# Output stores of a gated-attention and expert kernel: from SyncE's queue to GpSimd's

## The chip, the cores and the metric

The kernel runs on one core of one Trainium2 chip. The metric is the device time of one execution in microseconds (us), lower is better; the number given is the median of several executions. Beside it there is one profiled execution, taken by the hardware profiler, from which all rows of this document come.

The engines are named as the profile names them: PE is TensorE (matmuls), PEld its weight loads, DVE is VectorE, ACT is ScalarE, POOL is GpSimd, SP is SyncE. SP and POOL each have a queue of DMAs of their own; the packets of both are moved by the core's 16 DMA engines.

## What is computed

Two stages, one behind the other, with B = 8 sequences of S = 3072 tokens, width D = 256, 64 score channels and an inner width of 1024:

```python
scores = (1.0 / S) * np.matmul(z, z.transpose(0, 2, 1))
attn = np.maximum(scores, 0.0) ** 2
x = (u * np.matmul(attn, v)).reshape(B * S, D)
h1, h2 = x @ w1, x @ w2
out = np.maximum(h1, h2) @ w_out          # float32, 24576 x 256
```

The kernel uses max(h1, h2) = relu(h1 - h2) + h2, so it needs one inner product with w1 - w2 and a folded matrix w2 @ w_out.

## The kernel before, in words

**Steps.** Each sequence has six groups of 512 query tokens (`G` = 4 blocks of 128). The 48 (sequence, group) pairs are the steps, numbered n = 0 to 47. A step computes score tiles (PE), relu (ACT or DVE) and square (ACT or DVE) into `a_sb`, and from them the product with v in PSUM banks `acc0` and `acc1`. Because the scores are symmetric, a tile computed for one group is turned by a DMA transpose on SP's queue (`aT<-a_sb`, helper `turn`, L277) and read by a later step of the same sequence. The products of steps 3 and up are Strassen-like: seven half-size products in place of eight, with sums made by DVE (`es`, `lf`, `gs`, `xs`, `e`).

**The order on PE within a step n >= 3** is written out by hand (L1336 to L1389): the output products of step n-3 (`LAG` = 3, L49), named `o` 0 to 3; the inner products of step n-2, named `da`/`db` 0 to 3; and the step's own products in two phases, X and Y, each in two halves: `Xa`, `Xb`, `Ya`, `Yb`, each running over the six groups. `o` 0 opens the step, `Xb` with `o` 3 lies in its middle, `db` 3 lies between `Ya` and `Yb`, and `Yb` ends it. Score tiles of later steps are laid in between.

**Marks.** PE works with two halves of its rows side by side; before the halves swap banks, PE has to wait for its own earlier matmuls. This goes by way of POOL: `mark` (L93) puts an instruction on POOL that waits for the newest matmul, and a later matmul waits for it (`fence`, L87). POOL's queue is in program order, so whatever stands ahead of a mark in that queue delays it, and PE with it. There are 384 marks. In a step the last ones are that of `da` 3 and that at the end of `Ya` (L720, awaited by the first `Yb`); the next one comes behind `o` 0 of the following step (L1048).

**Loads** of u, v and z (`load`, L106) are DMAs of POOL's queue, in two parts of 64 rows each, 128 KB apiece for u and v. Each part waits for a chosen place in PE's order (`spot`, L1624): 0 is the first group of `Xa`, 1 that of `Xb`, 2 `da` 2, 3 the first group of `Ya`, 4 `db` 3, 5 the last group of `Yb`. In two steps of each sequence the two parts of the next u stand at places 4 and 5 (`U_SPOTS`, L1621).

**The output of a step** is made in `add_seven` (L968) for n = 3 to 46: ACT writes `o_sb` (L1078) after `o` 1, DVE and ACT finish it after `o` 3 (`oe0` on DVE by L296, `oe2` on ACT by L293), and job `store` (L1091) sends 512 KB, 128 partitions of 4 KB, to `out`. All this happens three steps after the step's own number. `o_sb` has two buffers (L74), so step n+2 writes the buffer that step n's store reads.

**The planner.** What runs on SP, POOL, ACT and DVE, and in which order, comes from a list scheduler (`find_orders`, L1861). Each `job` has the engines that may run it with a cost, jobs it depends on (`deps`), jobs that must only have begun (`after`), buffers it takes and uses, and a due time worked back from PE's order (`find_dues`). `share_wide` (L1938) gives the large tiles (`a_sb`, `aT`) their slots by the planned times. The planner's order is then written out and kept (`pin`).

Of the kernel before, what the change touches and what calls it, by code (L numbers as in the profile page):

```python
# [11 lines left out]
def kernel(  # L12
# [17 lines left out]
    nc = tc.nc  # L30
# [11 lines left out]
    G = 4  # L42
# [6 lines left out]
    LAG = 3  # L49
# [29 lines left out]
    pin = tc.keep_in_program_order  # L79
# [22 lines left out]
    def sp_dma(**kw):  # L102
        pin(nc.sync.dma_start(**kw))
# [134 lines left out]
    def tile_of(pool, key):  # L238
        return bufs[pool, key].tile
# [25 lines left out]
    steps = [Step(n, *divmod(n, NG)) for n in range(B * NG)]  # L265
# [702 lines left out]
    def add_seven(st):  # L968
        n, b, c = st.n, st.b, st.s
        xT, ok, sk, xk = ("xT", n), ("o", n), ("gs", n), ("xs", n)  # L970
# [109 lines left out]
        for name, ways, fn, deps, after, new, uses in (  # L1080
# [9 lines left out]
        out_b = out[ds(b * S, S), :].rearrange("(p t) d -> p t d", p=P)  # L1090
        job(  # L1091
            ("store", n),
            {"SP": 1300},
            lambda _: sp_dma(out=out_b[:, ds(c * G, G), :], in_=tile_of(*ok)),
            deps=[("oe2", n), ("oe0", n)],
            uses=[ok],
            lag=3000,
        )


    def add_second(st, split):
# [110 lines left out]
        if st.seven:  # L1212
            add_seven(st)
            return
# [92 lines left out]
    last = len(steps) - 1  # L1307
# [123 lines left out]
    for name in "s20 a10 s21 b10 a11 a12 b11 a13 s22 b12 b13 s23 a00 a01 s10 b00 b01 s11 a02 a03 b02 b03 s12 o00 s13 o01 o02 o03".split():  # L1431
        n, i = last - int(name[1]), int(name[2])
# [121 lines left out]
    def at_step(b, s, us):  # L1554
        return pe_job_at(starts[NG * b + s] + us * 1000)
# [121 lines left out]
    for dc in range(KD):  # L1677
# [7 lines left out]
            after=[("w2T", 0)] if dc else (),  # L1685
# [8 lines left out]
        after=at_step(0, 2, 6),  # L1694
# [390 lines left out]
```

## Time and profile before

| | |
|---|---|
| median of 3 executions | 885.39 us (884.83 to 885.87) |
| the profiled execution's own time | 889.46 us |
| its span, first to last instruction | 887.7 us |
| mean granted TensorE clock over the span | 0.998 |
| matmuls, marks, stores from SP | 16589, 384, 51 |

The profiled execution's own time is 1.76 us more than its span: 889.46 - 887.7. The profile is read from the engine that has no idle time, here PE, to the waits of the others.

### The profile page before, as it was taken

To read this page: it belongs to the slowest core of one execution; us is meant where nothing else is said; L and a number is where in the kernel's file an instruction comes from. 1 tells how busy PE (TensorE), PEld (TensorE's weight loads), DVE (VectorE), ACT (ScalarE), POOL (GpSimd) and SP (SyncE) were. 2 spreads that over 40 slices of the span, in tenths; PEclk is the share of its full clock that TensorE was granted. 3 is DMA by queue.
4 is the path that set the end of the run, shared out by engine and by line. 5 is a ranking of instruction groups with operands and counts; after the bars stand their busy time and mean duration, and the time that the engine had idled before them with its cause. 6 is when DMAs were issued, how large, how long until landed. Compare 5 with 4: busy or idle time off the path is not lost.

```text
span 887.7 us, 37934 instructions
## 1 busy us (share of the span) xinstructions
PE 879.5 (99%) x16589; PEld 718.3 (81%) x16589; DVE 804.6 (91%) x1721; ACT 753.0 (85%) x951; POOL 105.5 (12%) x218
## 2 busy tenths in 40 slices
PE   9999999999999999999999999999999999999998
PEld 4468888888888888788888888888888887788886
DVE  6877799999999999889999999999999999999984
ACT  8967998899978999689997899978999799987634
POOL 2101101111011110011101111011101111000000
PEclk9999999999999999999999999999999999999999
DMA  9999999997999989999999998999999999996621
GB/s 157 190 141 175 216 189 187 187 185 130 177 175 200 163 132 177 168 187 166 135 183 173 203 158 138 185 178 197 156 145 170 181 181 168 172 178 118 115 74 73
DMA packets 382310, 146.18 MB, mean 165 GB/s; under 512 B 360640, under 2 KB 362304, under 8 KB 382144
## 3 DMA queue, kind: packets, MB, share of 16 engines
q1 hardware_dynamic: 364128, 114.01, 79.4%
q0 software_dynamic: 18016, 29.75, 24.5%
q8 instruction: 129, 2.11, 1.0%
q14 instruction: 37, 0.30, 0.1%
HBM read 59.77 MB, written 25.17 MB: 96 GB/s over the span
## 4 chain that ended last, share of the span: by engine, by line
PE 97%; DVE 1%; DMA 1%; issue 0%; ACT 0%; POOL 0%; POOLq 0%; ACTq 0%
PE acc L86 50%; PE s_ps L86 47%; DMA z_sb<-in_z_dram 1%; ACT g_sb L282 0%; DVE zT L130 0%; DVE gs L299 0%; PE tpz_c L129 0%; ACT w2T_sb L293 0%; PE w2t_ps L1674 0%; DVE e L296 0%; DVE e L299 0%; DVE o_sb L296 0%; DVE w2T_sb L293 0%; DVE o_sb L299 0%; ACT o_sb L293 0%
## 5 line engine op out<-in xcount | busy, mean ns | idle before, releaser
L86 PEld LDWEIGHTS <-v_sb 64*128 64x128 bf16 x4552 | 327.9, 94 | 68.1 <-issue 4.3
L282 ACT ACTIVATE a_sb<-s_ps 128x1024 bf16<-128x1024 f32 (+1 forms) x334 | 302.2, 941 | 29.5 <-PE s_ps L86 26.3
L86 PEld LDWEIGHTS <-lf 64*128 64x128 bf16 x3240 | 260.1, 94 | 21.3 <-POOLq L94 3.3
L86 PE MATMUL acc<-es,v_sb 64*128 64x256 bf16 x2160 | 275.5, 269 | 0.0
L86 PE MATMUL acc<-es,lf 64*128 64x256 bf16 x1080 | 245.7, 269 | 0.0
L86 PE MATMUL acc<-a_sb,lf 64*128 64x256 bf16 x1224 | 229.8, 269 | 0.2 <-issue 0.2
L86 PE MATMUL s_ps<-xT,w_sb 64*128 64x512 bf16 (+1 forms) x1504 | 211.3, 377 | 0.1
L288 ACT ACTIVATE a_sb<-a_sb 128x1024 bf16<-128x1024 bf16 (+1 forms) x224 | 206.9, 953 | 1.5
L282 ACT ACTIVATE g_sb<-s_ps 128x1024 bf16<-128x1024 f32 x187 | 185.8, 1022 | 18.9 <-PE s_ps L86 16.8
L86 PE MATMUL acc<-aT,lf 64*128 64x256 bf16 x936 | 175.8, 269 | 0.0
L86 PE MATMUL acc<-a_sb,v_sb 64*128 64x256 bf16 (+2 forms) x1424 | 139.2, 284 | 0.3
L86 PE MATMUL s_ps<-zT 64*128 64x512 bf16 (+2 forms) x774 | 117.8, 333 | 0.3 <-DVE zT L130 0.2
L86 PEld LDWEIGHTS <-gs 64*128 64x128 bf16 x2816 | 100.1, 94 | 13.4 <-issue 3.1
L296 DVE TENSOR_TENSOR es<-aT 128x1536 bf16<-128x1536 bf16 (+1 forms) x117 | 106.2, 930 | 0.6
L107 POOL DMA_DIRECT2D u_sb<-in_u_dram x92 | 47.6, 517 | 430.6 <-PE acc L86 262.9
L86 PEld LDWEIGHTS <-w_sb 64*128 64x128 bf16 (+1 forms) x1520 | 74.2, 94 | 28.3 <-issue 1.7
L86 PEld LDWEIGHTS <-g_sb 64*128 64x128 bf16 x2304 | 85.8, 94 | 11.5 <-POOLq L94 7.4
L299 DVE TENSOR_TENSOR es<-a_sb 128x512 bf16<-128x512 bf16 x198 | 78.3, 419 | 17.1 <-PE acc L86 16.1
L290 DVE TENSOR_TENSOR a_sb<-a_sb 128x1024 bf16<-128x1024 bf16 (+1 forms) x112 | 74.2, 669 | 17.8 <-ACT a_sb L282 17.6
L86 PE MATMUL s_ps<-wf_sb,gs 64*128 64x128 bf16 x2112 | 84.6, 216 | 2.0 <-issue 1.9
L86 PE MATMUL acc<-aT,v_sb 64*128 64x256 bf16 x936 | 85.3, 269 | 0.0
L107 POOL DMA_DIRECT2D v_sb<-in_v_dram x89 | 46.1, 520 | 247.4 <-PE acc L86 133.8
(94 smaller groups left out, 1186.2 us busy)
## 6 DMA issues: line engine op xcount, KB each, us to landing
out_dram<-o_sb SPq DMA_DIRECT2D x47, 512.0 KB, 4.7
u_sb<-in_u_dram POOLq DMA_DIRECT2D x88, 128.0 KB, 4.2
v_sb<-in_v_dram POOLq DMA_DIRECT2D x82, 128.0 KB, 4.2
aT<-a_sb SPq DMA_TRANSPOSE x228, 5.0
z_sb<-in_z_dram POOLq DMA_DIRECT2D x12, 192.0 KB, 5.0
v_sb<-in_v_dram POOLq DMA_DIRECT2D x7, 256.0 KB, 6.8
u_sb<-in_u_dram POOLq DMA_DIRECT2D x4, 256.0 KB, 6.5
w_sb<-in_moe_w_dram POOLq DMA_DIRECT2D x2, 512.0 KB, 6.5
```

The source lines that it names most:

```text
L86: newest[0] = pin(nc.tensor.matmul(*args, **kw)).ins
L107: dma = pin(nc.gpsimd.dma_start(**kw))
L282: pin(nc.scalar.activation(out_ap, in_ap, AF.Relu))
L288: pin(nc.scalar.activation(ap, ap, AF.Square))
L290: pin(nc.vector.tensor_mul(ap, ap, ap))
L296: pin(nc.vector.tensor_add(*args))
L299: pin(nc.vector.tensor_sub(*args))
```

## The change

Three lines of the job `store` in `add_seven`. For steps with n + 3 < 47, that is n = 3 to 43, the store's engine is POOL instead of SP, so the DMA is issued by `nc.gpsimd`. It depends on the same two jobs as before; in addition it may be planned only once the second group of `Yb` of step n + 3 has begun in the plan. That is a rule for the planned order alone: the built DMA waits for no matmul. The stores of n = 44 to 46, of the three first steps and of the last step stay with SP.

```diff
         job(
             ("store", n),
-            {"SP": 1300},
-            lambda _: sp_dma(out=out_b[:, ds(c * G, G), :], in_=tile_of(*ok)),
+            {"POOL" if n + LAG < last else "SP": 1300},
+            lambda eng: pin((nc.gpsimd if eng == "POOL" else nc.sync).dma_start(out=out_b[:, ds(c * G, G), :], in_=tile_of(*ok))),
             deps=[("oe2", n), ("oe0", n)],
             uses=[ok],
+            after=[("Yb", n + LAG, steps[n + LAG].groups[1])] if n + LAG < last else [],
             lag=3000,
         )
```

In the built program 41 stores of 51 stand in POOL's queue and 10 in SP's. The order of all instructions on PE, DVE and ACT is the same as before, and so is the order of POOL's loads; on SP, besides the stores that left, two transposes of one early step have changed places. Some `a_sb` and `aT` tiles lie in other slots, because the planned times moved. On POOL each moved store stands directly behind the mark that ends `Ya`, or behind the load part that waits for `db` 3 where there is one, and ahead of the mark of the next step's `o` 0.

## Prediction

> **What bounds the kernel now.** I read the page first: which engine has no idle time, and what the DMA queues carry.
>
> ```profile
> span 887.7 us, 37934 instructions
> PE 879.5 (99%) x16589; PEld 718.3 (81%) x16589; DVE 804.6 (91%) x1721; ACT 753.0 (85%) x951; POOL 105.5 (12%) x218
> q1 hardware_dynamic: 364128, 114.01, 79.4%
> q0 software_dynamic: 18016, 29.75, 24.5%
> q8 instruction: 129, 2.11, 1.0%
> ```
>
> PE is busy 879.5 of 887.7 us; POOL is busy for 12%. SP's DMAs are queue q1, POOL's are q0, and q8 is the fetch of instructions: 129 packets, 2.11 MB, on the same DMA engines. A busy PE need not be a PE at its peak, so the second view is the table of waits:
>
> ```profile
> PE s_ps L86 <- issue: 1.9, 1, 1.9
> PE acc L86 <- issue: 0.2, 1, 0.2
> PEld L86 <- POOLq L94: 13.2, 77, 0.2
> DVE es L299 <- DMA aT<-a_sb: 1.0, 1, 1.0
> ```
>
> Behind the first few microseconds PE is idle hardly at all, and never for a DMA, a store or a turn; its longest idle time, 1.9 us, waits for nothing that the profile shows ("issue"). The marks cost weight loads 0.2 us at most. Of DVE's waits for turned tiles one is left, 1.0 us. Whether PE keeps its own pace is seen in the third view, the chain of waits in order of time. One run of 56 products comes once in each step at the same place:
>
> ```profile
> 226.91 2.84 PE s_ps L86 x56
> 334.52 2.84 PE s_ps L86 x56
> 371.66 1.92 issue
> 445.60 2.84 PE s_ps L86 x56
> 552.91 2.84 PE s_ps L86 x56
> 660.22 2.84 PE s_ps L86 x56
> 678.38 2.84 PE s_ps L86 x56
> 786.65 2.84 PE s_ps L86 x56
> ```
>
> These are starts, and neighbours are a sequence (six steps) apart, but for 660.22 to 678.38, which is one step. 445.60 to 552.91 and 552.91 to 660.22 are both 107.31 us, to the last digit. 226.91 to 334.52 is 107.61, 0.30 more; 678.38 to 786.65 is 108.27, 0.96 more; 334.52 to 445.60 is 111.08, 3.77 more, and there stands the 1.92 us of "issue". Behind it the granted clock falls:
>
> ```profile
> 373.60:377.00 3.40, 3.40 (x34) 1.97 (x36) 2.20 (x7) 2.13 (x3) 0.00 (x0) 0.53 1.13 212
> ```
>
> 3.40 us at a clock of 0.53 lose 3.40 x 0.47 = 1.60 us; with 1.92 that is 3.52 of the 3.77. So the steady part runs at PE's own pace with 0.30 + 3.77 + 0.96 = 5.03 us on top. The profiled execution's own time is 889.46; without the 3.77 it is 885.69, which is 0.30 above the median of 885.39. I take it that the timed executions lack this one stall. Without all 5.03 us it would be 884.43: the change can win about 885.39 - 884.43 = 0.96 us, unless it shortens the head or PE's own work, which it does not touch.
>
> **Part 1, what leaves SP.** 41 of 51 stores leave SP's queue.
>
> ```profile
> L103 SPq DMA_DIRECT2D out_dram<-o_sb x51: 332/518/1510, 87.8 to 884.6; - x51
> out_dram<-o_sb SPq DMA_DIRECT2D x47, 512.0 KB, 4.7
> ```
>
> Each took SP a median 0.518 us to issue and 4.7 us to land; 41 x 0.518 = 21 us of SP's time go, and the turns behind a store that waits for its output move up. Worth: 0. It would be worth something if PE, or an engine that holds PE up, waited for a turn; the only such wait is DVE's 1.0 us above, and PE's row has none. Bounds: no loss, and a gain of up to the 0.96 us above if all that is over the pace comes from the stores. I take 0, because nothing names them.
>
> **Part 2, what POOL gains.** 41 issues of 512 KB, 128 rows of 4 KB. No such DMA is in the trace, so the nearest rows are POOL's loads:
>
> ```profile
> L107 POOL DMA_DIRECT2D u_sb<-in_u_dram x92: 515/515/583, 4.2 to 848.0; - x92
> L107 POOL DMA_DIRECT2D v_sb<-in_v_dram x89: 515/515/599, 2.1 to 748.9; - x89
> L107 POOL DMA_DIRECT2D w_out_sb<-in_moe_w_out_dram x1: 894/894/894, 33.9 to 33.9; - x1
> w_out_sb<-in_moe_w_out_dram POOLq DMA_DIRECT2D x1, 512.0 KB, 7.7
> v_sb<-in_v_dram POOLq DMA_DIRECT2D x7, 256.0 KB, 6.8
> ```
>
> The issue costs 0.515 (64 rows of 4 KB) to 0.894 us (1024 rows of 1 KB). Seven of the v loads have the store's 128 rows and lie within the 0.599 maximum, so I take 0.6, or 41 x 0.6 = 25 us on an engine that idles 782. Landing takes 6.8 to 7.7 us by the 256 and 512 KB loads; I take 7.
>
> What waits behind the store on POOL is the mark of the next step's `o` 0, and PE waits for that mark. The store itself waits for DVE's last sum and ACT's last copy of its output. One step in full, for the store of n = 18; the second row counts marks in the window 397.5 to 402.4 and gives the first and the last:
>
> ```profile
> 395.99 0.41 DVE L296 TENSOR_TENSOR o_sb<-o_sb,s_ps 128x256 f32<-128x256 f32 x1
> L94 POOLq EVENT_SEMAPHORE  x2: 17/17/17, 397.9 to 402.3; - x2
> 398.63 0.52 POOL L107 DMA_DIRECT2D u_sb<-in_u_dram  x1 [2.96 <-PE s_ps L86]
> 402.06 0.60 PE L86 MATMUL s_ps<-xT,w_sb 64*128 64x512 bf16 x4
> L293 ACT COPY o_sb<-s_ps x2: 372/372/372, 393.6 to 411.5; 128x256 f32<-128x256 f32 x2
> L1078 ACT ACTIVATE o_sb<-s_ps x2: 597/597/597, 403.5 to 421.5; 128x512 f32<-128x512 f32 x2
> ```
>
> ACT is done at 393.6 + 0.37, DVE at 396.40, POOL reaches the store at 398.63 + 0.52 = 399.15. So the store finds both ready and leaves at once, early in `Yb`. It is done at 399.75; `o` 0 ends and `da` 0 starts at 402.06, and the mark follows at 402.3. Until 402.06 there are 2.91 us for an issue of 0.6. The margin is narrowest at the last moved store, n = 43 (first row below: POOL's load ends at 845.89, `da` 0 starts at 848.35: 2.46 us). The output is ready latest, against POOL, at the first, n = 3: DVE ends it at 124.93, 1.07 before the mark at 126.0 that stands ahead of the store.
>
> ```profile
> 845.37 0.52 POOL L107 DMA_DIRECT2D u_sb<-in_u_dram  x1 [13.38 <-PE s_ps L86]
> 848.35 0.59 PE L86 MATMUL s_ps<-xT,w_sb 64*128 64x512 bf16 x4
> 124.52 0.41 DVE L296 TENSOR_TENSOR o_sb<-o_sb,s_ps 128x256 f32<-128x256 f32 x1
> L94 POOLq EVENT_SEMAPHORE  x2: 17/17/17, 126.0 to 130.3; - x2
> ```
>
> So the marks come as before: 0. The cover is PE's own work in `Yb` and `o` 0; without it each store would cost its 0.6 us, 25 us in all. The store reads its `o_sb` from 399.75 to about 407; ACT writes that buffer again two steps on, at 421.5: 0.
>
> A rule of the Trainium skill speaks against this move. "SBUF — State Buffer", section "SBUF: two separate sides", says that descriptors of DMAs issued from GpSimd are written by its own cores, and that VectorE in a two-port mode locks them out; the same page's example has 620 ns become about 3100. By it the issue might take 0.6 x 5 = 3.0 us, past the 2.46. The trace does not bear it out here: beside a DVE that is busy 91%, none of 181 loads of u and v took over 0.599 us.
>
> **Part 3, the transfers.** The same 21 MB move on the same engines, but beside the turns instead of between them. In two steps a sequence, the second part of the next u is issued on POOL's queue some 2 us behind the store, and SP's `uT` waits for it. Behind a 512 KB store it may land up to 7 us later; `uT` and the turns behind it then go later. In the step above:
>
> ```profile
> uT<-u_sb SPq DMA_TRANSPOSE x48, 5.1
> 406.18 1.23 SPq L103 DMA_TRANSPOSE uT<-u_sb  x1
> 421.41 0.69 DVE L303 SCALAR_TENSOR_TENSOR xT<-e,uT 128x512 bf16<-128x512 f32 x1
> ```
>
> At worst `uT` starts at 413.2 and lands at 418.3, still 3.1 us ahead of DVE's use of it at 421.41. I take 0. Bounds: 0, and 3 us at each of these 14 steps, if turns behind a late `uT` became what PE waits for. The tiles in other slots get their data from the same instructions in the same order; I cost that at 0 too, covered by the same lack of waits on PE.
>
> **Sum.** 889.46 + 0 + 0 + 0 = 889.46 with this execution's stall, 885.69 without; against the median, 885.39 + 0, or **885.4 us**.
>
> **Rivals.**
>
> *A, instructions come late (slower).* The "issue" stall at 371.66 is what a late fetch on q8 would look like: PE stands still, no semaphore is awaited, and q8's 16 KB packets (2.11 MB / 129) share engines with q0 and q1. A store on q0 puts a third busy queue beside the turns and the fetch, 41 times for some 7 us. It decides from the point at which a fetch comes after PE has used up what it holds. Price: 3.77 us each, as measured. One in the median execution gives 885.39 + 3.77 = 889.2. For it: the stall exists, at a moment when the DMA engines were loaded. Against it: one in 129 fetches, although loads on q0 already meet turns everywhere. Chance 0.13.
>
> "DMA: Bandwidth & Descriptors", section "Queues, rings and completion order", of the Trainium skill says that each DMA engine goes round the queues that have work, packet by packet: a third one lengthens a fetch's wait. "Runtime: NRT & Kernel Launch", section "Instruction fetch mechanics", calls the cost of such a block mostly hidden, which 128 of 129 packets here agree with.
>
> *B, marks behind the store (slower).* If an issue takes more than 2.9 us in most steps, each excess goes to PE 41 times: at 3.3 us, 41 x 0.4 = 16 us, 902. Against it: 0.599 at most. Chance 0.05.
>
> *C, late u (slower).* 14 x 1 us gives 899. Against it: no DMA wait on PE. Chance 0.03.
>
> *D, the stall goes (faster).* If the timed executions too hold a stall of 3.77 us and the store on SP brings it on, the time falls to 885.39 - 3.77 = 881.6. Against it: 885.69 fits the median without it. Chance 0.05.
>
> That the change does not do what it says is excluded: in the built order 41 stores are POOL's.
>
> **How the numbers follow.** The forecast has 0.74. Its own range is 884.4 (all 0.96 won) to 886.4 (as much lost again to small fetch waits). 0.74 is not enough for the range, so it reaches on to A: 884.4 to 889.2, with 0.87. A difference of 0.2%, 1.8 us, is about what a measurement can tell from none: 883.6 to 887.2. Faster is D, 0.05; slower is A, B and C, 0.21; the same, 0.74.
>
> **What would show it.** In the profile after: 41 POOL rows `out_dram<-o_sb` of about 0.6 us; the wait for L94 still at 0.2 us at most; runs of 56 products 107.31 us apart; POOL near 130 us. A: new "issue" waits on PE, with a fallen clock behind them. B: store rows over 2.4 us and longer waits for L94. C: waits of SP for u beyond 407 and PE or ACT waiting for `aT`. D: an execution without any "issue" wait and well under 884. I am wrong if PE has a row of waits that is not in the list above.

## The result, and the profile after

The changed kernel takes 891.51 us (median of 13 executions, 887.62 to 900.1) against 886.55 for the kernel before on the same chip (13 executions, 884.15 to 891.89): a ratio of 1.0058, 95% interval 1.0039 to 1.0077. It is slower by 0.58%, some 5 us. The forecast was 885.4, and 891.5 lies above the range (884.4 to 889.2). Of the 6.1 us between them 1.2 are the start of the sum: it began at 885.39, the median of three executions of the kernel before, and thirteen give 886.55. The intervals in this document are over undisturbed executions; a profile is one execution, so a single pause in it is a draw.

The changed kernel's profiled execution took 890.09 us. First its page:

```profile
span 888.3 us, 37957 instructions
PE 877.8 (99%) x16589; PEld 741.8 (84%) x16589; DVE 804.8 (91%) x1721; ACT 753.6 (85%) x951; POOL 128.9 (15%) x259
q1 hardware_dynamic: 358224, 92.52, 73.4%
q0 software_dynamic: 23920, 51.25, 29.9%
q8 instruction: 129, 2.11, 1.0%
out_dram<-o_sb POOLq DMA_DIRECT2D x41, 512.0 KB, 5.2
```

21.5 MB have gone from q1 to q0, and POOL's busy time rose from 105.5 to 128.9 us: 23.4 us for 41 issues. A row of the groups by line shows them alone:

```profile
L1094 POOL DMA_DIRECT2D out_dram<-o_sb x41: 566/566/575, 127.7 to 845.5; - x41
```

0.57 us each, as reckoned (0.6). The waits of TensorE and its weight loads, in the same execution:

```profile
PE acc L86 <- DVE e L296: 1.3, 1, 1.3
PE s_ps L86 <- issue: 1.0, 2, 0.7
PE acc L86 <- issue: 0.6, 2, 0.4
PE acc L86 <- POOLq L94: 0.3, 1, 0.3
PEld L86 <- POOLq L94: 13.7, 78, 0.5
PEld L86 <- issue: 13.3, 36, 1.6
```

Where before had one "issue" wait of 1.9 us and one of 0.2 there are four small ones, one mark that comes late by 0.3 to 0.5 us, and one sum of DVE. The DVE wait lies at 112.75 us, before the first moved store (127.7), and up to there the order on every queue is as before. Behind it stands a load of v:

```profile
DVE lf L296 <- DMA v_sb<-in_v_dram: 1.2, 1, 1.2
```

That load landed 8.2 us behind its issue, 4.2 us in before's profile. PE stands at the same place, for 0.5 to 1.7 us, in nine of the twenty profiles of this case, one of them with all stores on SyncE's queue. So no moved store is its direct cause, but how often it comes in executions without a profile is not known. TensorE's pace is read from the chain, as before:

```profile
228.73 2.84 PE s_ps L86 x56
336.56 2.84 PE s_ps L86 x56
437.15 4.79 issue
444.37 2.84 PE s_ps L86 x56
553.05 2.84 PE s_ps L86 x56
660.52 2.84 PE s_ps L86 x56
768.04 2.84 PE s_ps L86 x56
```

Before, a sequence without pauses took 107.31 us. Now they take 107.83, 107.81, 108.68, 107.47 and 107.52: every sequence has lost something, 2.76 us in all five. In before's profile two sequences were clean and one held the 3.77 us pause. The second of the five, 107.81, is the late mark: the 4.79 us in this chain is POOL's queue standing still at 437.15, ahead of it. The other four lose it in small pauses.

One part of the loss is in no row of TensorE's waits. The last matmuls of the chain and the longest DRAIN of POOL's queue (the three numbers with slashes are the shortest, the median and the longest, in ns), first before, then after:

```profile
877.09 7.11 PE s_ps L86 x120
L2080 POOLq DRAIN  x3: 40/101/6357, 878.5 to 887.4; - x3
```

```profile
876.43 7.11 PE s_ps L86 x120
L2081 POOLq DRAIN  x3: 46/93/9701, 877.8 to 888.1; - x3
```

The DRAIN stands at the end of POOL's program, and the end of the kernel waits for it. Before, it was over at 878.5 + 6.36 = 884.9, ahead of the last output packet (886.0). Now it lasts until 887.5, 2.2 us behind the last packet (885.3). From PE's last matmul to the end of the span it takes 887.7 - 884.2 = 3.5 us before and 888.3 - 883.5 = 4.8 us after: 1.3 us of the 5.

### The profile page after: what moved, and what is told of

Read it like the earlier page. It is cut to its first block, busy times and chain, and to the rows that moved or that the text cites. A ratio compares the mean times of both kernels' runs of the same rounds, so it can differ in the third digit from the quotient of the medians.

```text
span 888.3 us, 37957 instructions
## 1 busy us (share of the span) xinstructions
PE 877.8 (99%) x16589; PEld 741.8 (84%) x16589; DVE 804.8 (91%) x1721; ACT 753.6 (85%) x951; POOL 128.9 (15%) x259
## 4 chain that ended last, share of the span: by engine, by line
PE 96%; DMA 1%; issue 1%; DVE 1%; ACT 0%; POOL 0%; POOLq 0%; DVEq 0%; ACTq 0%
PE acc L86 49%; PE s_ps L86 46%; DMA v_sb<-in_v_dram 1%; DMA z_sb<-in_z_dram 0%; ACT g_sb L282 0%; DVE zT L130 0%; DVE gs L299 0%; PE tpz_c L129 0%; ACT w2T_sb L293 0%; PE w2t_ps L1675 0%; DVE e L296 0%; DVE o_sb L296 0%; ACT o_sb L293 0%; DVE w2T_sb L293 0%; DVE o_sb L299 0%
## 5 line engine op out<-in xcount | busy, mean ns | idle before, releaser
L86 PEld LDWEIGHTS <-v_sb 64*128 64x128 bf16 x4552 | 339.9, 94 | 59.7 <-issue 5.8
L86 PEld LDWEIGHTS <-lf 64*128 64x128 bf16 x3240 | 269.7, 94 | 16.8 <-POOLq L94 3.3
L86 PE MATMUL acc<-es,v_sb 64*128 64x256 bf16 x2160 | 274.9, 269 | 0.0
L86 PE MATMUL acc<-es,lf 64*128 64x256 bf16 x1080 | 245.0, 269 | 0.0
L86 PE MATMUL acc<-a_sb,lf 64*128 64x256 bf16 x1224 | 234.8, 269 | 0.0
L86 PE MATMUL s_ps<-xT,w_sb 64*128 64x512 bf16 (+1 forms) x1504 | 215.7, 376 | 0.1
L86 PE MATMUL acc<-aT,lf 64*128 64x256 bf16 x936 | 180.3, 269 | 0.0
L86 PE MATMUL acc<-a_sb,v_sb 64*128 64x256 bf16 (+2 forms) x1424 | 142.6, 284 | 2.2 <-DVE e L296 1.3
L86 PE MATMUL s_ps<-zT 64*128 64x512 bf16 (+2 forms) x774 | 123.3, 333 | 0.4 <-DVE zT L130 0.4
L86 PEld LDWEIGHTS <-gs 64*128 64x128 bf16 x2816 | 103.9, 94 | 10.3 <-issue 2.2
L86 PEld LDWEIGHTS <-w_sb 64*128 64x128 bf16 (+1 forms) x1520 | 83.2, 94 | 23.7 <-POOLq L94 1.5
L86 PEld LDWEIGHTS <-g_sb 64*128 64x128 bf16 x2304 | 88.3, 94 | 10.2 <-POOLq L94 7.4
L86 PE MATMUL acc<-aT,v_sb 64*128 64x256 bf16 x936 | 88.7, 269 | 0.3 <-issue 0.3
L86 PE MATMUL s_ps<-wf_sb,gs 64*128 64x128 bf16 x2112 | 86.3, 216 | 1.1 <-issue 1.0
```

Of the source, the lines that this page charges most:

```text
L86: newest[0] = pin(nc.tensor.matmul(*args, **kw)).ins
```

## The experiments

Three theories stood from the start, and S beside them: F (instruction fetches come late), G (POOL's own queue is held and its marks or loads go out late), L (loads of u and v land late behind the store), S (what the new plan moves along). Each run was timed beside the kernel before on the same chip, and its ratio is to that; the groups of runs are on four different chips.

### Same plan and place, another queue or none

Only the issuing line differs; the planned order stays that of the changed kernel. The third version leaves 41 of the 51 outputs unwritten.

```diff
-pin((nc.gpsimd if eng == "POOL" else nc.sync).dma_start(...))
+sp_dma(...)                                                       # SyncE
+pin((nc.scalar if eng == "POOL" else nc.sync).dma_start(...))     # ScalarE
+None if eng == "POOL" else sp_dma(...)                            # no store
+[pin(... .dma_start(...)) for _ in range(2 if eng == "POOL" else 1)]   # twice
```

> The plan of the changed kernel, and the 41 moved stores at the same place of it, but issued by SyncE's queue (q1) in place of GpSimd's (q0). F (instruction fetches on q8 come late beside a third busy ring): ratio to the kernel before 0.998 to 1.002. G (GpSimd's own queue is held, by a lane's semaphore or the store's landing, and its marks or loads go out late): 0.998 to 1.002. L (loads of u and v land late behind the store's packets on q0): 0.998 to 1.002. S (not the queue but what the new plan moves along: the order of SyncE's turns, the slots of a_sb and aT, and the store's place): 1.004 to 1.008, as the changed kernel.

> The same plan and place, the 41 stores issued by ScalarE's queue: a ring beside q0 and q1, and nothing of it on GpSimd. F: 1.004 to 1.008, for the third ring is there as before. G and L: 0.998 to 1.002 (41 issues on ScalarE, idle for 15% of the span, at most 0.002 more). S: 1.004 to 1.008.

> The plan of the changed kernel with the 41 moved stores left out, so that the outputs of all but the last steps are never written: the floor of this plan, with 41 x 512 KB less on the queues. F, G and L: 0.996 to 1.000. S by the order of turns and the slots: 1.004 to 1.008.

> The changed kernel with each of the 41 moved stores issued twice in a row by GpSimd (the same bytes to the same place): twice the bytes and twice the issues in the same stretches. F, G and L: the loss doubles or more, 1.009 to 1.020. S: 1.004 to 1.008, as with one store.

| stores | us, median | ratio to before | 95% interval |
|---|---|---|---|
| SyncE | 886.58 | 0.9996 | 0.9981 to 1.0011 |
| ScalarE | 895.37 | 1.0082 | 1.0048 to 1.0116 |
| none | 884.58 | 0.9976 | 0.9960 to 0.9992 |
| GpSimd, twice | 1030.74 | 1.1596 | 1.1547 to 1.1644 |

S falls: the same plan with the stores on SyncE's queue costs nothing. G and L cannot explain the run on ScalarE, where POOL has no store and q0 none of its bytes, and the loss is as large or larger. The run without stores is 2.4 us below the kernel before, so more was to be won than the prediction's 0.96. ScalarE's waits on TensorE, all that are not in the first microseconds:

```profile
PE acc L86 <- issue: 4.3, 3, 3.1
PE s_ps L86 <- issue: 2.2, 3, 1.6
PEld L86 <- issue: 17.3, 38, 3.3
PEld L86 <- POOLq L94: 13.2, 77, 0.2
```

and those of the kernel without the stores, which has no "issue" wait on PE at all:

```profile
PEld L86 <- POOLq L94: 13.1, 77, 0.2
PEld L86 <- issue: 8.6, 28, 0.4
```

The weight loads' row is a gauge of one execution, not of a kernel: 8.6 us in 28 waits is what remains with no pause, 17.3 is ScalarE's queue, 13.3 the changed kernel, and before's own profile, 2.9 us above its median, had 13.6. The marks stand at 0.2 us in both, so ScalarE's loss is waiting for instructions and nothing else that the table names. Matmul for matmul, its profile falls 10.9 us behind the one without pauses that is shown further below; nine such pauses, with the 3.4 us of half clock behind the longest, make 10.2 of them.

The doubled store was meant as a double dose and is something else. The second store goes to the same place and waits for the first to land. Waits of POOL and of PE in that run:

```profile
POOL out_dram L1094 <- DMA out_dram<-o_sb: 209.0, 41, 7.2
```

```profile
PE s_ps L86 <- POOLq L94: 102.4, 41, 4.9
```

POOL stands 209.0 / 41 = 5.10 us behind each first store; with the two issues of 0.57 and 0.54 us the mark is held for 6.2 us, and PE waits 102.4 / 41 = 2.50 us for it: about 3.7 us are absorbed. Part 2 of the prediction read a slack of 2.46 to 2.91 us, up to the start of `da` 0, so PE needs the mark a little later than that. This is rival B's mechanism. In the changed kernel an issue of 0.57 us stays well inside the slack. The rest of the 144 us is in the main the clock: its mean is 0.967 here, over 1021.2 us.

### The same kernel again, and the bytes taken apart

> The changed kernel as it is, for a second time and a second profile on the chip that takes the next three. All theories: ratio 1.004 to 1.008. F expects TensorE's pauses again behind fetches that were asked for 1 to 2.5 us before a moved store's first packet; G expects its waits for GpSimd's marks to add up to most of the loss.

The second series gave 892.09 us and 1.0055 (1.0029 to 1.0082). Its profile holds one long pause. The chain, the windows (us; busy time and instructions of PE, PEld, DVE, ACT, POOL; granted clock; DMA share; GB/s) and the DMA queues of 493 to 498 us:

```profile
496.75 0.10 PE acc L86
496.85 2.77 issue
499.62 1.47 PE acc L86 x23
```

```profile
496.50:500.00 3.50, 0.73 (x17) 0.51 (x13) 3.50 (x9) 2.52 (x6) 0.52 (x1) 1.00 1.11 121
```

```profile
q1 hardware_dynamic: 1543, 0.39, 110.9%
q0 software_dynamic: 113, 0.41, 24.0%
q8 instruction: 1, 0.02, 2.8%
```

DVE is busy through all of it; TensorE stands. One packet of instructions moved in these 5 us and took 2.8% of 16 x 5 us = 2.24 us. In the trace it ends at 498.08, and PE goes on at 499.62. A pause of this kind can be told by two marks: PE resumes mostly 1.2 to 1.7 us behind the end of such a packet, and always near the same place in its program, 91 to 94 matmuls into a block of 128 (129 packets of 16 KB for 16589 matmuls, each with its weight load, are about 128 matmuls a packet). All seven small pauses of the first profile that are not the DVE sum and the late mark bear both.

G was to show as waits for marks worth most of the loss. The row is 13.7 us against 13.2, one mark late by 0.5 us, at the place around 441 us where the chain above has POOL standing 4.79 us. It returns in both profiles of the changed kernel, so the late mark is worth about 0.5 us of the 5. It stands 4 to 8 us behind the 128th DMA of POOL's queue. In all eleven profiles with 239 DMAs on that queue a mark at that place is late by 0.9 to 2.3 us, whatever the bytes, and so is one in the quarters below; in the seven profiles with 198 DMAs, as before, no mark is. The DRAIN goes with that number too, not with the bytes: 9.70 us in all eleven (9.86 in the quarters), 6.36 us in all seven. So being issued by GpSimd costs the changed kernel 1.3 + 0.5 = 1.8 us of the 5, the 1.3 of them wherever the stores stand. Executions without a profile agree: of all series with the stores on GpSimd's queue the lowest is 886.06 us, while before, SyncE's, ScalarE's away from the loads (below) and the one without stores reach 883.92 to 885.30.

What the profiled executions took over 884.49 us, the one without pauses, in us; a part is read by comparing the start of every matmul, and up to 0.5 us is not in the table:

| profile | over | late instructions | end | mark | load of v |
|---|---|---|---|---|---|
| before | 5.0 | 5.0 | 0 | 0 | 0 |
| changed kernel | 5.6 | 3.0 | 1.3 | 0.5 | 1.3 |
| changed, second series | 8.2 | 4.7 | 1.3 | 0.5 | 1.5 |

Before's profile had as much waiting for instructions as these two, so profiles alone do not show that the change adds any; the medians and the runs that follow have to.

Next, each moved store in two parts by partition:

```diff
+[(nc.gpsimd, ds(0, r)), (nc.sync, ds(r, P - r))]      # r = 8 or 64
```

> The plan of the changed kernel; at each of the 41 places GpSimd stores 8 of the 128 partitions (32 KB) and SyncE the other 120. GpSimd has all 41 issues and waits, its queue hardly any bytes. F and L: 0.998 to 1.003. G: 1.004 to 1.008, as the changed kernel.

> The same with 64 partitions (256 KB) on each queue. F: between none and all, 1.001 to 1.006 (half the backlog on the second queue). G: 1.004 to 1.008, as with 8 partitions and with 128. L: 1.001 to 1.006.

With 8 of 128 partitions on POOL: 889.83 us, 1.0020 (0.9998 to 1.0042). With 64: 888.77, 1.0020 (0.9995 to 1.0045). All 41 issues are there in both, and what is left, 0.0020 or 1.8 us, is as much as the later end and the late mark, both of which their profiles show. So G as the main cause falls, and the other 3.2 us need the whole stores. The two runs cannot be told from each other, nor surely from 1, so there is no dose curve.

### The moment of the fetch, which fell

A first reading of the changed kernel's trace seemed to show the mechanism: each of its seven pauses followed a fetch asked for 0.9 to 2.4 us ahead of a moved store's first packet. So the stores were tied to chosen matmuls, with a table of 41 rows, once clear of the fetches and once in their way.

```diff
+STORE_AT = {3: ('Yb', 6, 0), 4: ('Xb', 8, 1), ...}
-{"POOL" if n + LAG < last else "SP": 1300},
+{"POOL" if n in STORE_AT else "SP": 1300},
+load(timed=True, out=..., in_=...)       # waits for the newest matmul
+after=[STORE_AT[n]] if n in STORE_AT else [],
```

> The moved stores stay on GpSimd's queue, but each is tied to a matmul chosen so that its first packet should start some 2 us BEFORE the next instruction fetch is asked for and at least 3 us after the last one (TensorE's instruction count gives the times: a fetch every 256 instructions; the table names one matmul a store). F: the collisions go, ratio 0.997 to 1.002. G and L: as many issues, bytes and loads on the same queue, and one more wait on it, 1.004 to 1.008 or more.

> The same table with the other phase: each moved store's first packet should start about 1.5 us AFTER a fetch is asked for (as in the seven pauses of the changed kernel). F: a pause at half or more of the 41 stores, of 0.2 to 1 us and a half clock behind the long ones: 1.012 to 1.040. G and L: as the run with the other phase, 1.004 to 1.008.

Clear gave 887.96 us, 1.0008 (0.9992 to 1.0023); in the way 890.27, 1.0035 (1.0015 to 1.0056), where F wanted 1.012 or more. The trace showed that the aim was off: first packets came 1.1 to 4.2 us behind the issue, not 1.6. A second pair was aimed by the issue.

> The run with the other phase missed its aim: there the stores were issued 4 to 7 us ahead of the fetch requests and their first packets came 1.1 to 4.2 us after the issue, not 1.6; in the two profiles of the changed kernel the late fetches are those asked for 0 to 2 us after a store's ISSUE (3.8 to 4.1 us on average from the request to the end, 2.8 elsewhere). So the table is made again by the issue: here each store is tied to a matmul so that a fetch is asked for just ahead of the issue (by some 0.5 us) and the next one is 5 us off. F, by the issue: ratio 0.997 to 1.002. G and L: 1.004 to 1.008. If the first packets decided after all, this is the bad phase: 1.005 or more.

> The same with the fetch asked for 1.0 to 1.6 us after each store's issue, with as many loads within 4 us ahead of the stores (19 against 18). F, by the issue: a quarter or more of 41 fetches late, 1.004 to 1.015, and the ratio clearly above that of the run asked for ahead of the issue. G and L: no difference between the two.

The supposedly good moment gave 1.0036 (1.0012 to 1.0060), the bad one 1.0015 (0.9995 to 1.0035). That is the wrong way round, though the intervals overlap, and the theory of the moment is dropped: seven pauses out of one profile had been read as a rule.

### Shorter bursts

```diff
+("Yb", N, groups[1]), ("Yb", N, groups[3]), ("Yb", N, groups[5]), ("o", n + 1, 1)   # 32 partitions at each
```

> Each moved store in four parts of 32 partitions (128 KB), tied to four matmuls 0.9 to 2 us apart, the first at the changed kernel's place: the same bytes on GpSimd's queue in short bursts, but 164 issues in place of 41. F: the bursts are a quarter as long, ratio 0.998 to 1.003. G: four times the issues and waits ahead of the marks, 1.006 to 1.020. L: as the changed kernel, 1.004 to 1.008.

1.0052 (1.0025 to 1.0078): no gain. F's forecast missed. G's lower bound is inside the interval, and so is L's whole forecast. The profile shows that four times the issues begin to cost, in two marks awaited by PE:

```profile
PE s_ps L86 <- POOLq L94: 2.3, 2, 1.4
```

### Near the loads and away from them

All four tables of the last section but one had lost less than the changed kernel. What they share is distance from POOL's loads: the changed kernel's place puts 31 of 41 stores 0.5 to 0.9 us behind a load of u, v or z. The next table counts, over 18 profiles (all but those of the doubled store and of the run asked for before the issue, an execution of 901 us), for every packet of instructions from 130 us on, which packets of stores and loads were moving between the moment it was asked for (taken as the 75th matmul behind a block's start) and its own start. It gives how many ended over 4.9 us after that moment, and at how many PE lost over 0.12 us against the execution without pauses (at five of these 64 the packet was early, and PE waited for something else; the one at "neither" is a late mark):

| in flight meanwhile | packets | over 4.9 us | PE paused |
|---|---|---|---|
| neither | 512 | 0 | 1 |
| a store, on any queue | 161 | 1 | 1 |
| a load | 1014 | 48 (5%) | 15 (1.5%) |
| a load, and a store on SyncE's queue | 107 | 11 (10%) | 6 (6%) |
| a load, and a store on GpSimd's or ScalarE's queue | 282 | 57 (20%) | 41 (15%) |

So the tables were made once more, by the loads: as far from them as may be, and beside them. On ScalarE's and SyncE's queues a place is one in the queue's order, with no wait for a matmul.

> The phase of the fetch requests fell as the cause: asked for ahead of the issue 1.0036, behind it 1.0015. What the four tables had in common, and what orders them, is how long a moved store is in flight together with a load of GpSimd's queue: 3.5, 4.8, 9.0 and 9.5 us in their profiles for 1.0008, 1.0015, 1.0036 and 1.0035, against 21 and 23 us for 1.0058 and 1.0055 in the changed kernel, whose place puts most stores 0.57 us behind a load. Here each store is tied to a matmul as far as may be from the loads (29 us of overlap by the plan, 81 in the changed kernel). B (a store beside a load makes one long stream on the second queue, and behind it come late fetches and marks): 0.998 to 1.002. P (chance placing, the four ratios no more than scatter about one mean of 1.0024): 1.002 to 1.006.

> The same table the other way round: each store at the matmul that gives the most time in flight together with loads (135 us by the plan). B: at least as much as the changed kernel, 1.005 to 1.015. P: 1.002 to 1.006, as the table away from the loads.

> The stores by ScalarE's queue again (1.0082 at the changed kernel's place), now at the places away from the loads, by the order of ScalarE's instructions and with no wait of their own. B: most of the loss goes, 0.999 to 1.004. If a third queue costs by its being there, wherever the store stands: 1.005 to 1.011.

> SyncE's queue again (0.9996 at the changed kernel's place), the stores at the places away from the loads in the plan: the version that could beat both, between the floor without stores (0.9976) and the kernel before. B: 0.997 to 1.000. P: 0.998 to 1.002.

| stores | us, median | ratio to before | 95% interval |
|---|---|---|---|
| GpSimd, away | 887.64 | 1.0014 | 0.9988 to 1.0041 |
| GpSimd, beside | 897.94 | 1.0127 | 1.0098 to 1.0156 |
| ScalarE, away | 888.49 | 1.0011 | 0.9991 to 1.0031 |
| SyncE, away | 884.91 | 0.9990 | 0.9970 to 1.0010 |

On ScalarE's queue the place alone takes 1.0082 to 1.0011, with the intervals apart. On GpSimd's, 1.0055 to 1.0058 becomes 1.0014, which is no more than the later end (1.3 us); the intervals overlap, but of the pairs of one execution of the changed kernel (24) and one of this one (12) the changed kernel's is the longer in 88%. The run beside the loads is too dear, in part by another mechanism, as the waits of PE and of ACT show (lines are 9 higher in these kernels, so L95 is L86):

```profile
PE s_ps L95 <- DVE o_sb L308: 5.1, 6, 1.8
PE acc L95 <- issue: 2.7, 3, 1.6
PE acc L95 <- POOLq L103: 1.3, 1, 1.3
```

```profile
ACT o_sb L1087 <- DMA out_dram<-o_sb: 5.5, 4, 2.1
```

Some stores stood so late that ACT's next use of their `o_sb` buffer waited for them to land, DVE for ACT, and PE for DVE. So the table was ended 5 us earlier in each step, and the run on SyncE's queue repeated.

> In the run beside the loads, 5.5 of its pauses were another thing: stores placed so late that the next use of their o buffer waited for them to land. Here the table beside the loads ends 5 us earlier in each step, so that this wait goes (118 us of overlap by the plan, 81 in the changed kernel, 29 away from the loads). B: 1.004 to 1.010, as much as the changed kernel or more, without waits of TensorE for o_sb. P: 1.000 to 1.004.

> SyncE's queue with the places away from the loads, a second time: is it faster than the kernel before? B: 0.997 to 1.000 again, and both series together clearly below 1. P: 0.999 to 1.002.

Beside, earlier: 890.47 us, 1.0036 (1.0014 to 1.0058), no wait for `o_sb`. It is below the 1.004 that B asked for, and inside P's range. It is slower than away in 81% of the pairs of executions, yet not slower than the changed kernel, although by the plan it had more overlap (118 us against 81). The overlap counted in the packets of its profile is smaller, 17.8 us. By that count (time in which a packet of a moved store and one of a load are both moving) the nine series with whole stores on GpSimd's queue, without the first one beside the loads and the doubled store, line up so:

| kernel | in flight together, us | ratio |
|---|---|---|
| phase clear | 4.0 | 1.0008 |
| away from loads | 4.8 | 1.0014 |
| asked after issue | 8.2 | 1.0015 |
| asked before issue | 12.8 | 1.0036 |
| phase hit | 15.3 | 1.0035 |
| beside, earlier | 17.8 | 1.0036 |
| changed kernel, two series | 28.1, 30.4 | 1.0058, 1.0055 |
| quarters | 38.2 | 1.0052 |

Each ratio holds about 0.0015 for the later end. The order is good, but it was found after most of the runs, and it is not a law for other queues: on SyncE's queue the changed kernel's place has 27.4 us of it and costs nothing, and ScalarE's two runs have 25.0 and 20.0 us with 1.0082 and 1.0011.

SyncE, away, gave 885.36 us the second time, 0.9982 (0.9962 to 1.0002). Its first profile is the pace itself. Chain, and weight loads:

```profile
227.21 2.84 PE s_ps L95 x56
334.52 2.84 PE s_ps L95 x56
441.83 2.84 PE s_ps L95 x56
549.14 2.84 PE s_ps L95 x56
656.45 2.84 PE s_ps L95 x56
763.76 2.84 PE s_ps L95 x56
```

```profile
PEld L95 <- issue: 8.7, 28, 0.4
```

All are 107.31 us apart, and that execution took 884.49 us. It is the best version here with all its outputs, but neither interval excludes 1, so it is not shown to be faster than the kernel before.

## Why the prediction was wrong, point by point

**What bounds the kernel** was right. PE's own pace sets the time; 884.43 us was reckoned for a kernel without pauses, and the two profiles without an "issue" wait on PE gave 884.57 (no stores) and 884.49. The gain left to win was about 2.1 us, not 0.96, because the median of three executions was 1.2 us too low.

**Part 1** (SP freed: 0) holds. With the same plan and the stores on SyncE the ratio is 0.9996, and nothing that moves up on SP shows in the time.

**Part 2** (POOL's issue: 0) failed for 1.8 of the 5 us. What it looked at holds: the issue is 0.566 to 0.575 us where 0.6 was taken, and the slack is at least the 2.46 to 2.91 us that it read. But it looked only at the marks right behind the stores. It left out the end of POOL's program, whose DRAIN grew from 6.36 to 9.70 us and moved the end by 1.3 us, and one mark late by 0.5 us behind the 128th DMA, where POOL stood 4.79 us. Why 41 more DMAs do this is not shown. The Trainium skill's rule in "SBUF — State Buffer", section "SBUF: two separate sides", that VectorE can lock out GpSimd's descriptor writing, did not decide the issues here: no store issue took over 0.575 us beside a DVE busy 91%.

**Part 3** (the transfers: 0) is the step that failed for the larger part, 5.0 - 1.8 = 3.2 us: that part is there with whole stores at the changed kernel's place, and goes when they are split between two queues or moved away from the loads. It looked for late data, in u, `uT` and turned tiles, and PE waits for none of those. What the transfers delay is the instructions themselves, and that was left to rival A. On ScalarE's queue this is nearly all of the loss in the profiled execution, which is the median one; on GpSimd's it is what the counts above support, and how much of the 3.2 us it makes is open.

**Rival A** had that mechanism and a wrong size. Its argument against itself was one pause among 129 fetches, read as rarity; but before's profile holds six of 0.2 us and more, five of them small ones inside the 0.30 and 0.96 us that the prediction left unexplained, and with a load and a store on a second queue in flight 15% of the fetches stop PE. It priced one pause of 3.77 us, with a fallen clock behind it. The changed kernel's two profiles show seven and three, of 0.2 to 3.0 us, and the granted clock stays at 1.00 behind all of them. That its total of 3.8 us comes near the 3.2 is luck. The Trainium skill calls a block's fetch "mostly hidden" ("Runtime: NRT & Kernel Launch", section "Instruction fetch mechanics"). With neither a store nor a load in flight the traces agree, none of 512 packets came late; with a load and a store on a second queue they do not.

**B, C and D** did not come. The margin of marks holds at 0.57 us and breaks at 6.2, as the doubled store shows; the one late mark is not a store's issue. PE waits for no u. No execution of the changed kernel took less than 887.62 us. The prediction's own sign of being wrong, a row of PE outside its list, did come (DVE's sum), but for a load of v ahead of any moved store.

**What stays open.** Shown is that the plan costs nothing; that issuing from GpSimd costs 1.8 us by the end and the mark; that whole stores on a second queue cost the rest, on GpSimd's as on ScalarE's; and, on ScalarE's queue, that PE spends it waiting for instructions and that the place of the stores decides. That nearness to a load is what makes a place bad is supported, not settled. So is the difference to SyncE's queue: beside a load its stores go with pauses at 6% of the packets, those on a second queue with 15%. The likely reason, that on SyncE's queue a store takes the place of a turn in an order that the queue keeps while on a second queue it comes on top of them, is argued, not measured.

## What to carry to other kernels

An engine that is never idle can still wait for its own instructions: where PE's only waits are "issue", count how near its fetches come to their limit, and treat every DMA that is moved to a second queue as a load on that fetch. A queue with idle time is not free capacity when the packets of all queues together already take about all the time of the 16 DMA engines (79.4 + 24.5 + 1.0% in before's page). When DMAs move to another engine, look at the end of that engine's program too, not only at what stands behind each of them. And one profile of a kernel with rare pauses is a draw: compare medians before its waits. If a large store must go to another queue, try first where it stands relative to that kernel's other transfers: here the place alone was worth 0.7% on ScalarE's queue, more than the choice of the engine.

## What the runs showed of the hardware that was not expected

- A 512 KB store costs nothing on the queue that already carries the turns (0.9996) and 0.6 to 0.8% on a queue beside it (1.0058 on GpSimd's, 1.0082 on ScalarE's), at the same place and with the same order of the other work on PE, DVE and ACT. On GpSimd's, 0.15% of it is the later end.
- GpSimd's last DRAIN took 6.36 us in seven profiles with 198 DMAs on its queue and 9.70 us in eleven with 239, and the end of the kernel waited for the longer one. A mark of that queue behind its 128th DMA was late in each of the eleven.
- A packet of instructions takes 1.0 us in the median to move once started; the one of the 2.77 us pause took 2.2. In the 18 profiles counted above, PE paused at 54 of the 62 packets that ended later than 1.2 us before it would have reached, at its pace, the 92nd matmul of the next block, and at 5 of the 1988 that ended over 1.6 us before; it resumed mostly 1.2 to 1.7 us behind the packet's end.
- In the changed kernel's two profiles a store's first packet came 1.2 to 5.3 us behind the start of its issue.
- Two DMAs to the same place in `out` are put one behind the other by a wait on their engine's queue: 5.10 us each on GpSimd's, and the time grew by 16%.
